# Last transform stage: four 64x64 quarters of the PE array and the plain 50 by 49 table, eight positions and 128 channels per call

## The chip, the cores and the metric

The kernel runs on one core of one Trainium2 chip. The metric is device time in microseconds (us); lower is better. A core has the matrix engine (PE, with its weight loads shown apart as PEld), the vector engine (DVE), the scalar engine (ACT), GpSimd (POOL), and SyncE (SP), whose queue issues the DMA transfers. PE reads SBUF and writes PSUM, from which ACT and DVE read.

## The reference

For each of 8 batches of 3136 positions by 256 channels, a real Fourier transform along the positions, a complex mix of the channels with a soft threshold, and the transform back; then a feed-forward block with a three-tap convolution and a gate.

```python
X = np.fft.rfft(x, axis=1)
Yr = Xr @ w_r - Xi @ w_i + b_r
Yi = Xr @ w_i + Xi @ w_r + b_i
Yr = np.sign(Yr) * np.maximum(np.abs(Yr) - 0.01, 0.0)      # Yi the same
y = np.fft.irfft(Yr + 1j * Yi, n=3136, axis=1)             # 8 x 3136 x 256
h = np.maximum(y @ w_in, 0.0)                              # 256 -> 1024
conv = sum(conv_w[k] * hp[:, k:k + 3136, :] for k in range(3))   # hp: h, one zero position each side
out = (h * sigmoid(conv)) @ w_out                          # 1024 -> 256
```

## The kernel before

3136 is 49 times 64, and the transform is done as two short ones, forward (stages 1 and 2) and back (stages 3 and 4). Stage 1 (L257, L274) and stage 2 (L301), the mix (L329), the threshold and stage 3 (L361) run first, for all batches, in about the first 535 us. Stage 3 leaves its result in DRAM: `sc2[b]` has 128 rows, 25 frequencies and 256 channels for batch b. Row 4j + 2o + c is position j (0 to 31) of half o (0 or 1), real (c = 0) or imaginary (c = 1).

Stage 4 (`stage4`, L502 to L516) is the last transform. For one j and one o it contracts 50 values (2 parts by 25 frequencies) with a fixed table of 50 by 49, which gives 49 output positions m; the position in the sequence is 64m + 32o + j. The kernel before does both halves o in one matmul: the table `i2` is 100 by 98 and block-diagonal (half of it is zero), and the stationary operand is `z2[:, j, 128 channels]`, 100 rows by 128 columns. A call covers four j and both halves of the channels: one transfer of 100 rows brings `z2` (L505), then 2 x 4 matmuls of 100 x 128 against 100 x 98 (L509) fill one PSUM bank per half of the channels, ACT casts the 784 results per partition to `yh` (L515), and DVE forms the rest `yl` (L516). A batch takes eight calls, all of them 64.

All matmuls of stages 1, 2 and 4 are plain fp32. In the trace each such matmul is two records on PE and two weight loads on PEld: stage 4 issues 512 matmuls and has 1024 records. The other matmuls are of split operands in fp32r (a high and a low part each), one record each.

Then the feed-forward block: 28 chunks of 896 positions, each in eight steps f of 128 hidden channels. `up` does 12 matmuls of 128 x 450 (L528), ACT and DVE make `gh` and `gl` from them (L530 to L543), and `down` does 21 matmuls of 128 x 256 (L556), four steps later. Stage 4 of batch 0 and two calls of batch 1 stand ahead of the first step; the other 54 calls are placed one at a time among the steps, by the loop's line `if todo and f in (1, 4, 7)`. `ps_s4` and `ps_h` share two PSUM buffers (tag `ps_h`), and `z2` has three buffers. From the feed-forward block on, and for stage 4, a scheduler with its own timeline orders the instructions of each engine; each engine then works in that order, and so does SP's queue.

Of the kernel before, what the change touches and what calls it, by code (L numbers as in the profile page):

```python
# [9 lines left out]
F32 = mybir.dt.float32  # L10
# [8 lines left out]
B, S, D, FF = 8, 3136, 256, 1024  # L19
R = 49  # L20
R2 = 64
U = 24
SP = 64
H = 32
# [5 lines left out]
P = 128  # L30
NT = D // P
# [4 lines left out]
def _tables():  # L36
    n = np.arange(R)
    n2 = np.arange(R2)
    u = np.arange(U + 1)

    f = np.zeros((R, 2, U + 1))
    ang = 2 * np.pi * ((n[:, None] * u[None, :]) % R) / R
    f[:, 0, :] = np.cos(ang)
    f[:, 1, :] = -np.sin(ang)
    fwd1 = np.zeros((R, 2, 2 * R))
    for h in range(2):
        for uu in range(1, U + 1):
            for c in range(2):
                fwd1[:, h, (uu - 1) * 4 + c * 2 + h] = f[:, c, uu]
        fwd1[:, h, 4 * U + h] = f[:, 0, 0]  # L50

    g = np.transpose(f, (1, 2, 0)).copy()
    g[:, 1:, :] *= 2.0
    g /= S
    g = np.roll(g, -1, axis=1)
    inv2 = np.zeros((2, 2 * (U + 1), R, 2))
    for i in range(2):
        inv2[i, :, :, i] = g.reshape(2 * (U + 1), R)
    fwd2 = np.zeros((2, R2, U + 1, 2, SP))
    inv1 = np.zeros((2, SP, U + 2, 2, R2))  # L60
    for uu in range(U + 1):
        at = (uu - 1) % (U + 1)
        for s in range(SP):
            k = uu + R * s
            th = 2 * np.pi * ((k * n2) % S) / S
            sn, cs = np.sin(th), np.cos(th)
            if uu == 0:
                if k > S // 2:
                    continue
                edge = k in (0, S // 2)  # L70
                if edge:
                    sn = np.zeros(R2)
                    cs = np.round(cs)
                w = 1.0 if edge else 2.0
                fwd2[0, :, at, 0, s] = cs
                fwd2[0, :, at, 1, s] = -sn
                inv1[0, s, at, 0, :] = w * cs
                inv1[1, s, at, 0, :] = -w * sn
            else:
                sg = 1.0 if k <= S // 2 else -1.0  # L80
                fwd2[0, :, at, 0, s] = cs
                fwd2[1, :, at, 0, s] = sn
                fwd2[0, :, at, 1, s] = -sn * sg
                fwd2[1, :, at, 1, s] = cs * sg
                inv1[0, s, at, 0, :] = cs
                inv1[0, s, at, 1, :] = sn
                inv1[1, s, at, 0, :] = -sg * sn
                inv1[1, s, at, 1, :] = sg * cs

    inv1[:, :, U + 1] = inv1[:, :, U]  # L90
    inv1[:, :, 1::2] = inv1[::-1, :, 1::2]

    return {
        "fwd1": fwd1.reshape(2 * R, 2 * R).astype(np.float32),
        "fwd2": fwd2.reshape(2 * R2, (U + 1) * 2 * SP).astype(np.float32),
        "inv1": inv1.reshape(2 * SP, U + 2, 2, 2, H).transpose(0, 1, 4, 3, 2).reshape(2 * SP, (U + 2) * 2 * R2).astype(np.float32),
        "inv2": inv2.reshape(4 * (U + 1), 2 * R).astype(np.float32),
    }


# [1 line left out]
def spectral_ffn_kernel(ctx: ExitStack, tc: tile.TileContext, x, w_r, w_i, b_r, b_i,  # L102
                        w_in, conv_w, w_out, fwd1, fwd2, inv1, inv2, out):
    nc = tc.nc
    K1, K2, KQ, KI = 2 * R, 2 * SP, 2 * R2, 4 * (U + 1)

    dram = ctx.enter_context(tc.tile_pool(name="dram", bufs=1, space=DRAM))
    sc1 = [dram.tile([K1, H, D], F32, name=f"sc1_{b}") for b in range(B)]
    sc2 = [dram.tile([KQ, U + 1, D], F32, name=f"sc2_{b}") for b in range(B)]

    cst = ctx.enter_context(tc.tile_pool(name="cst", bufs=1))


    i2 = cst.tile([KI, 112], F32, name="i2")[:, 0:K1]
    cw = cst.tile([P, 3, NF], F32, name="cw")
    win = [cst.tile([P, NT, FF], F32R, name=f"win_{q}") for q in range(2)]
    wout = [cst.tile([P, NF, D], F32R, name=f"wout_{q}") for q in range(2)]
# [363 lines left out]
    def pool(name, bufs=1, **kw):  # L481
        return ctx.enter_context(tc.tile_pool(name=name, bufs=bufs, reuse_waits="tile", **kw))

    zio, y_a = pool("zio", 3), pool("y_a")
# [3 lines left out]
    wk.tile([P, 24], F32, name="pad", bufs=1)  # L488
    psh, pso = pool("psh", 2, space=PSUM), pool("pso", space=PSUM)

    JG = 4
    NPC = H // JG

    def new_y(b):
        y = [(y_a, y_b)[b % 2].tile([P, NT, SW], F32R, name=nm) for nm in ("yh", "yl")]
        for q in y:
            qf = q.bitcast(F32)
            nc.vector.memset(qf[:, :, 0:1], 0.0)
            nc.vector.memset(qf[:, :, S + 1:S + 2], 0.0)
        return y  # L500

    def stage4(b, jg, y):  # L502

        z2 = zio.tile([KI, JG, D], F32, name="z2")
        nc.sync.dma_start(z2, sc2[b].rearrange("(j q) u e -> (q u) j e", q=4)[:, jg * JG:(jg + 1) * JG, :])  # L505
        ps = psh.tile([P, NT, 512], F32, name="ps_s4", tag="ps_h")
        for t in range(NT):
            for j in range(JG):
                nc.tensor.matmul(ps[:, t, j * K1:(j + 1) * K1], z2[:, j, t * P:(t + 1) * P], i2, start=(j == 0), stop=(j == JG - 1),  # L509
                                 skip_group_check=True)  # L510
        src = ps[:, :, 0:JG * K1].rearrange("p t (j m) -> p t m j", j=JG)

        def view(q):
            return q[:, :, 1:S + 1].rearrange("p t (m j) -> p t m j", j=H)[:, :, :, jg * JG:(jg + 1) * JG]
        nc.scalar.copy(view(y[0]), src)  # L515
        nc.vector.tensor_tensor(view(y[1]), src, view(y[0].bitcast(F32)), op=ALU.subtract)  # L516

    def up(f, halves):
        ps = psh.tile([P, 2, 512], F32, name="ps_h", tag="ps_h")
        w = slice(f * P, (f + 1) * P)  # L520
        for a, (y, c0) in enumerate(halves):
            mm = []
            for t in range(NT):
                mm.append((win[0][:, t, w], y[0][:, t, c0:c0 + CH + 2]))
                mm.append((win[0][:, t, w], y[1][:, t, c0:c0 + CH + 2]))
                mm.append((win[1][:, t, w], y[0][:, t, c0:c0 + CH + 2]))
            for n, (lt, rh) in enumerate(mm):
                nc.tensor.matmul(ps[:, a, 0:CH + 2], lt, rh, start=(n == 0), stop=(n == len(mm) - 1))  # L528
        h = hp.tile([P, 2, CH + 2], F32, name="h")
        nc.scalar.activation(h, ps[:, :, 0:CH + 2], AF.Relu)  # L530
        c = wk.tile([P, 2, CH], F32, name="c", bufs=3)
        if f in TAP_DVE:
            nc.vector.tensor_scalar_mul(c, h[:, :, 0:CH], cw[:, 0, f:f + 1])
        else:
            nc.scalar.mul(c, h[:, :, 0:CH], cw[:, 0, f:f + 1])  # L535
        for k in (1, 2):
            nc.vector.scalar_tensor_tensor(c, h[:, :, k:k + CH], cw[:, k, f:f + 1], c, op0=ALU.mult, op1=ALU.add)  # L537
        nc.scalar.activation(c, c, AF.Sigmoid)  # L538
        nc.vector.tensor_tensor(c, h[:, :, 1:CH + 1], c, op=ALU.mult)  # L539
        gh = wk.tile([P, 2, CH], F32R, name="gh", bufs=5)  # L540
        gl = wk.tile([P, 2, CH], F32R, name="gl", bufs=5)
        nc.scalar.copy(gh, c)  # L542
        nc.vector.tensor_tensor(gl, c, gh.bitcast(F32), op=ALU.subtract)  # L543
        return [q.rearrange("p a n -> p (a n)") for q in (gh, gl)]
# [32 lines left out]
    ys = {0: new_y(0)}  # L577
    for jg in range(NPC):
        with tc.high_priority(offset=HP):
            stage4(0, jg, ys[0])  # L580
    ys[1] = new_y(1)
    for jg in range(2):
        stage4(1, jg, ys[1])
    todo = [(1, jg) for jg in range(2, NPC)]
    gs, accs = {}, None
    n_st = NCH * NF
    for st in range(n_st + LAG):
        if st < n_st:
            ci, f = divmod(st, NF)
            hv = [divmod(2 * ci + a, NH) for a in range(2)]  # L590
            if f == 0:
                nb = hv[1][0] + 1
                if nb < B and nb not in ys and hv[0][0] == hv[1][0]:
                    ys[nb] = new_y(nb)
                    todo = [(nb, jg) for jg in range(NPC)]
            gs[st] = up(f, [(ys[b], a * CH) for b, a in hv])
            if todo and f in (1, 4, 7):
                b, jg = todo.pop(0)
                stage4(b, jg, ys[b])
        if st >= LAG:  # L600
            ci, f = divmod(st - LAG, NF)
            accs = down(ci, f, gs.pop(st - LAG), accs)
# [24 lines left out]
```

## Time and profile before

| | |
|---|---|
| median of 3 runs | 1760.06 us (1758.44 to 1760.09) |
| the profiled execution | 1759.99 us, span 1758.2 us, mean granted clock 0.990 |
| PE busy | 1721.6 us (98%) |
| DVE, ACT busy | 1472.0 us (84%), 1206.8 us (69%) |
| stage 4 on PE (L509) | 1024 records, busy 128.0 us; first 522.1 us, last 1568.4 us |
| stage 4 on ACT (L515), DVE (L516) | 64 each, 65.9 us and 67.4 us |
| loads of `z2` | 64 transfers of 400 KB |

The span runs from the first to the last instruction; the execution's own time is 1.8 us more. The matmuls overlap each other, so that the mean time of one (281 ns for stage 4) is far more than what one adds: the step from one start to the next is what counts. "x" is the number of records in a group. In the chain of waits a line of PE with "x16" is a stretch of so many records, with the time that they took.

### The profile page before, as it was taken

To read this page: it belongs to the slowest core of one execution; us is meant where nothing else is said; L and a number is where in the kernel's file an instruction comes from. 1 tells how busy PE (TensorE), PEld (TensorE's weight loads), DVE (VectorE), ACT (ScalarE), POOL (GpSimd) and SP (SyncE) were. 2 spreads that over 40 slices of the span, in tenths; PEclk is the share of its full clock that TensorE was granted. 3 is DMA by queue.
4 is the path that set the end of the run, shared out by engine and by line. 5 is a ranking of instruction groups with operands and counts; after the bars stand their busy time and mean duration, and the time that the engine had idled before them with its cause. 6 is when DMAs were issued, how large, how long until landed. Compare 5 with 4: busy or idle time off the path is not lost.

```text
span 1758.2 us, 28865 instructions
## 1 busy us (share of the span) xinstructions
PE 1721.6 (98%) x11872; PEld 1602.2 (91%) x11872; DVE 1472.0 (84%) x1757; ACT 1206.8 (69%) x1565; POOL 118.7 (7%) x54
## 2 busy tenths in 40 slices
PE   5999999999999999999999999999999999999999
PEld 2788888888988999999999999999999999999998
DVE  2778988889995988888888888888888888888887
ACT  2567677677665777677777777777777777777766
POOL 0122222222230000000000000000000000000000
PEclk8999999999998999999999999999999999999999
DMA  7877777767434110111111011111101111100001
GB/s 223 256 233 240 226 230 237 232 204 234 141 104 126 42 48 22 41 50 50 41 50 50 22 40 50 50 40 50 50 22 41 50 50 41 50 22 22 22 22 43
DMA packets 108305, 165.48 MB, mean 94 GB/s; under 512 B 8492, under 2 KB 86316, under 8 KB 108174
## 3 DMA queue, kind: packets, MB, share of 16 engines
q1 hardware_dynamic: 108174, 163.64, 29.4%
q8 instruction: 94, 1.54, 0.4%
q14 instruction: 37, 0.30, 0.1%
HBM read 86.02 MB, written 77.59 MB: 93 GB/s over the span
## 4 chain that ended last, share of the span: by engine, by line
PE 93%; DMA 2%; DVE 2%; issue 1%; ACT 0%; SPq 0%; DVEq 0%; ACTq 0%
PE ps_h L528 31%; PE acc L556 31%; PE ps_mx L329 11%; PE ps_s L509 6%; PE ps_s L257 5%; PE ps_s L301 5%; PE ps_s L361 3%; DMA t<-in_fwd_dram 1%; DMA z<-sc 1%; DVE v L337 0%; DMA sc<-a 0%; DVE p L333 0%; DMA sc<-ha 0%; DVE fl L307 0%; DVE v L348 0%
## 5 line engine op out<-in xcount | busy, mean ns | idle before, releaser
L556 PE MATMUL acc<-wout,gh 128*128 128x256 f32 x3136 | 567.4, 280 | 0.0
L528 PE MATMUL ps_h<-yh,win 128*128 128x450 f32 x1792 | 550.6, 368 | 0.0
L537 DVE SCALAR_TENSOR_TENSOR c<-h,cw,c 128x896 f32<-128x896 f32 x448 | 512.9, 1147 | 38.9 <-ACT c L535 37.3
L556 PEld LDWEIGHTS acc<-wout,gh 128*128 128x128 f32 x3136 | 490.1, 188 | 5.1
L556 PE MATMUL acc<-wout,gl 128*128 128x256 f32 x1568 | 437.4, 280 | 0.0
L530 ACT ACTIVATE h<-ps_h 128x900 f32<-128x900 f32 x224 | 207.4, 926 | 261.1 <-PE ps_h L528 261.1
L528 PEld LDWEIGHTS ps_h<-yh,win 128*128 128x128 f32 x1792 | 339.4, 189 | 26.1 <-DVE yl L516 0.4
L528 PE MATMUL ps_h<-yl,win 128*128 128x450 f32 x896 | 329.7, 368 | 0.0
L543 DVE TENSOR_TENSOR gl<-c,gh 128x896 fp32r<-128x896 f32 x224 | 243.0, 1088 | 76.3 <-ACT gh L542 74.7
L556 PEld LDWEIGHTS acc<-wout,gl 128*128 128x128 f32 x1568 | 293.8, 188 | 0.6
L539 DVE TENSOR_TENSOR c<-h,c 128x896 f32<-128x896 f32 x224 | 243.1, 1086 | 48.2 <-ACT c L538 48.2
L542 ACT CAST gh<-c 128x896 fp32r<-128x896 f32 x224 | 211.0, 942 | 70.2 <-DVE c L539 68.3
L538 ACT ACTIVATE c<-c 128x896 f32<-128x896 f32 x224 | 213.0, 951 | 8.2 <-DVE c L537 4.4
L329 PE MATMUL ps_mx<-wmix_hi,fl 128*128 128x256 f32 x600 | 185.2, 309 | 2.8 <-DVE fl L311 2.8
L329 PE MATMUL ps_mx<-wmix_hi,fh 128*128 128x256 f32 x600 | 183.7, 306 | 0.7 <-DVE v L337 0.6
L528 PEld LDWEIGHTS ps_h<-yl,win 128*128 128x128 f32 x896 | 169.4, 189 | 11.0
L535 ACT ACTIVATE c<-h,cw 128x896 f32<-128x896 f32 x168 | 176.1, 1048 | 2.2 <-DVE gl L543 0.2
L329 PE MATMUL ps_mx<-wmix_lo,fh 128*128 128x256 f32 x600 | 168.6, 281 | 0.0
L351 POOL TENSOR_TENSOR sl<-v,sh 128x1024 fp32r<-128x1024 f32 x50 | 118.5, 2370 | 410.7 <-PE ps_s L361 254.1
L337 DVE TENSOR_TENSOR v<-ps_mx,p 64x512 f32<-64x512 f32 x200 | 137.4, 687 | 2.9
L301 PEld LDWEIGHTS ps_s<-t,a 128*128 128x128 f32 (+1 forms) x800 | 99.7, 198 | 39.6 <-issue 28.8
L509 PEld LDWEIGHTS ps_s<-i,z 100*128 100x128 f32 x1024 | 128.1, 198 | 5.8 <-issue 3.0
(84 smaller groups left out, 1959.2 us busy)
## 6 DMA issues: line engine op xcount, KB each, us to landing
z<-sc SPq DMA_DIRECT2D x64, 400.0 KB
xr<-in_x_dram SPq DMA_DIRECT2D x63, 392.0 KB
a<-sc SPq DMA_DIRECT2D x48, 512.0 KB
sc<-z SPq DMA_DIRECT2D x48, 512.0 KB
out_dram<-o SPq DMA_DIRECT2D x27, 896.0 KB
sc<-a SPq DMA_DIRECT2D x56, 392.0 KB
sc<-ha SPq DMA_DIRECT2D x8, 392.0 KB
win_bits<-in_moe_w_in_dram SPq DMA_DIRECT2D x4, 512.0 KB
```

The source lines that it names most:

```text
L301: nc.tensor.matmul(ps[:, k], a2[0:rows, k, t * P:(t + 1) * P], t2[0:rows, u, :], start=(k == 0), stop=(k == UG - 1), skip_group_check=True)
L329: nc.tensor.matmul(ps[c][:, k, :], lt, rh, start=(n == 0), stop=(n == len(mm) - 1))
L509: nc.tensor.matmul(ps[:, t, j * K1:(j + 1) * K1], z2[:, j, t * P:(t + 1) * P], i2, start=(j == 0), stop=(j == JG - 1), skip_group_check=True)
L528: nc.tensor.matmul(ps[:, a, 0:CH + 2], lt, rh, start=(n == 0), stop=(n == len(mm) - 1))
L530: nc.scalar.activation(h, ps[:, :, 0:CH + 2], AF.Relu)
L535: nc.scalar.mul(c, h[:, :, 0:CH], cw[:, 0, f:f + 1])
L537: nc.vector.scalar_tensor_tensor(c, h[:, :, k:k + CH], cw[:, k, f:f + 1], c, op0=ALU.mult, op1=ALU.add)
L538: nc.scalar.activation(c, c, AF.Sigmoid)
L539: nc.vector.tensor_tensor(c, h[:, :, 1:CH + 1], c, op=ALU.mult)
L542: nc.scalar.copy(gh, c)
L543: nc.vector.tensor_tensor(gl, c, gh.bitcast(F32), op=ALU.subtract)
L556: nc.tensor.matmul(acc[m // 2][:, m % 2, :], lt[:, sl], rh[:, f, :], start=(f == 0 and n == 0 and m % 2 == 0), stop=(f == NF - 1 and n == ...
```

## The change

Stage 4 uses the table once, 50 by 49, held twice in SBUF: in partitions 0 to 49 and in 64 to 113. A call now covers eight j and one half of the channels (128), so that a batch still has eight calls. `z2` has half o = 0 in partitions 0 to 49 and o = 1 in 64 to 113, and is brought by two transfers of 50 rows. For each j there are four matmuls: for each half o (rows 0 or 64 on) and each 64 of the 128 channels (PSUM partitions 0 or 64 on), 50 x 64 against 50 x 49. Each thus names one quarter of the array. A call has 32 matmuls in place of 8. Half o = 0 writes one PSUM bank and o = 1 the other. The casts and the differences still have 784 elements per partition, in runs of eight in place of four.

```diff
-    inv2 = np.zeros((2, 2 * (U + 1), R, 2))
-    for i in range(2):
-        inv2[i, :, :, i] = g.reshape(2 * (U + 1), R)
+    inv2 = np.zeros((2, R2, R))
+    inv2[:, 0:2 * (U + 1)] = g.reshape(2 * (U + 1), R)
...
-    i2 = cst.tile([KI, 112], F32, name="i2")[:, 0:K1]
+    i2 = cst.tile([P, 112], F32, name="i2")[:, 0:R]
...
-    JG = 4
-    NPC = H // JG
+    JG = 8
+    NPC = H // JG * NT
...
-    def stage4(b, jg, y):
-
-        z2 = zio.tile([KI, JG, D], F32, name="z2")
-        nc.sync.dma_start(z2, sc2[b].rearrange("(j q) u e -> (q u) j e", q=4)[:, jg * JG:(jg + 1) * JG, :])
-        ps = psh.tile([P, NT, 512], F32, name="ps_s4", tag="ps_h")
-        for t in range(NT):
-            for j in range(JG):
-                nc.tensor.matmul(ps[:, t, j * K1:(j + 1) * K1], z2[:, j, t * P:(t + 1) * P], i2, start=(j == 0), stop=(j == JG - 1),
-                                 skip_group_check=True)
-        src = ps[:, :, 0:JG * K1].rearrange("p t (j m) -> p t m j", j=JG)
+    def stage4(b, n, y):
+
+        js, t = slice(n // NT * JG, (n // NT + 1) * JG), n % NT
+        z2 = zio.tile([P, JG, P], F32, name="z2")
+        z2v = sc2[b].rearrange("(j o c) u e -> o (c u) j e", o=2, c=2)
+        for o in range(2):
+            nc.sync.dma_start(z2[o * R2:o * R2 + KI], z2v[o, :, js, t * P:(t + 1) * P])
+        ps = psh.tile([P, 2, 512], F32, name="ps_s4", tag="ps_h")
+        for j in range(JG):
+            for o in range(2):
+                rows = slice(o * R2, o * R2 + KI)
+                for c in range(2):
+                    half = slice(c * R2, (c + 1) * R2)
+                    nc.tensor.matmul(ps[half, o, j * R:(j + 1) * R], z2[rows, j, half], i2[rows, :], start=(j == 0), stop=(j == JG - 1),
+                                     skip_group_check=True)
+        src = ps[:, :, 0:JG * R].rearrange("p o (j m) -> p o m j", j=JG)
```

The order of PE in the middle of the feed-forward block, before: `ps_s` is `ps_s4`, `acc` the output of `down`, and "x8" eight equal instructions in a row.

```order
L528 MATMUL ps_h<-yh,win_79 128x450
L528 MATMUL ps_h<-yh,win_78 128x450
L528 MATMUL ps_h<-yl,win_78 128x450
L528 MATMUL ps_h<-yh,win_79 128x450
L509 MATMUL ps_s_12473<-i_76,z_12471 128x98 x8
L556 MATMUL acc_12224<-wout_80,gl 128x256
L556 MATMUL acc_12225<-wout_80,gh 128x256
```

The same place in the changed kernel (L514 was L509, L533 was L528, L561 was L556):

```order
L533 MATMUL ps_h<-yh,win_79 128x450
L533 MATMUL ps_h<-yh,win_78 128x450
L533 MATMUL ps_h<-yl,win_78 128x450
L533 MATMUL ps_h<-yh,win_79 128x450
L514 MATMUL ps_s_12640<-i_76,z_12637 64x49 x32
L561 MATMUL acc_12397<-wout_80,gh 128x256
L561 MATMUL acc_12397<-wout_81,gh 128x256
```

A call is still one stretch without other matmuls in it, now of 32, between matmuls that name the whole array. In both kernels the 64 calls make 57 such stretches: three ahead of the feed-forward block, of two, two and six calls, and 54 of one call.

The order of SP's queue in the same part, before (`z` is `z2`, `sc_2` the result of stage 3 for batch 2):

```order
L505 DMA z_7527<-sc_2_67 100x4x256
L569 DMA out_dram<-o 128x7x256
L505 DMA z_7684<-sc_2_67 100x4x256
L505 DMA z_7839<-sc_2_67 100x4x256
L569 DMA out_dram<-o 128x7x256 x2
L505 DMA z_7944<-sc_2_67 100x4x256
```

And in the changed kernel (L507 was L505, L574 was L569):

```order
L507 DMA z_7927<-sc_2_67 50x8x128 x2
L574 DMA out_dram<-o 128x7x256
L507 DMA z_8109<-sc_2_67 50x8x128 x2
L507 DMA z_8289<-sc_2_67 50x8x128 x2
L574 DMA out_dram<-o 128x7x256 x2
L507 DMA z_8419<-sc_2_67 50x8x128 x2
```

Each load of `z2` is two issues in place of one, at the same place of the queue between the stores of the output.

More of the change, by code (lines that the diff above doesn't have):

```diff
@@ L96, in _tables @@
         "inv1": inv1.reshape(2 * SP, U + 2, 2, 2, H).transpose(0, 1, 4, 3, 2).reshape(2 * SP, (U + 2) * 2 * R2).astype(np.float32),
-        "inv2": inv2.reshape(4 * (U + 1), 2 * R).astype(np.float32),
+        "inv2": inv2.reshape(P, R).astype(np.float32),
     }
@@ L104, in spectral_ffn_kernel @@
     nc = tc.nc
-    K1, K2, KQ, KI = 2 * R, 2 * SP, 2 * R2, 4 * (U + 1)
+    K1, K2, KQ, KI = 2 * R, 2 * SP, 2 * R2, 2 * (U + 1)
     dram = ctx.enter_context(tc.tile_pool(name="dram", bufs=1, space=DRAM))
@@ L500, in new_y @@
         return y
-    def stage4(b, jg, y):
-        z2 = zio.tile([KI, JG, D], F32, name="z2")
-        nc.sync.dma_start(z2, sc2[b].rearrange("(j q) u e -> (q u) j e", q=4)[:, jg * JG:(jg + 1) * JG, :])
-        ps = psh.tile([P, NT, 512], F32, name="ps_s4", tag="ps_h")
-        for t in range(NT):
-            for j in range(JG):
-                nc.tensor.matmul(ps[:, t, j * K1:(j + 1) * K1], z2[:, j, t * P:(t + 1) * P], i2, start=(j == 0), stop=(j == JG - 1),
-                                 skip_group_check=True)
-        src = ps[:, :, 0:JG * K1].rearrange("p t (j m) -> p t m j", j=JG)
+    def stage4(b, n, y):
[13 more added lines that the diff above has]
+        src = ps[:, :, 0:JG * R].rearrange("p o (j m) -> p o m j", j=JG)
         def view(q):
-            return q[:, :, 1:S + 1].rearrange("p t (m j) -> p t m j", j=H)[:, :, :, jg * JG:(jg + 1) * JG]
+            return q[:, t, 1:S + 1].rearrange("p (m o j) -> p o m j", o=2, j=H)[:, :, :, js]
         nc.scalar.copy(view(y[0]), src)
```

## The prediction

> **What bounds the kernel now.** I began with the busy shares and the chain of work that ended last.
>
> ```profile
> PE 1721.6 (98%) x11872; PEld 1602.2 (91%) x11872; DVE 1472.0 (84%) x1757; ACT 1206.8 (69%) x1565; POOL 118.7 (7%) x54
> ...
> PE 93%; DMA 2%; DVE 2%; issue 1%; ACT 0%; SPq 0%; DVEq 0%; ACTq 0%
> PE ps_h L528 31%; PE acc L556 31%; PE ps_mx L329 11%; PE ps_s L509 6%; PE ps_s L257 5%; PE ps_s L301 5%; PE ps_s L361 3%; DMA t<-in_fwd_dram 1%; DMA z<-sc 1%; DVE v L337 0%; DMA sc<-a 0%; DVE p L333 0%; DMA sc<-ha 0%; DVE fl L307 0%; DVE v L348 0%
> ```
>
> PE makes 93% of the chain, and stage 4 (L509) 6% of it, about 105 us. Whether that holds where stage 4 runs is read from the stretches of the span: ahead of the feed-forward block, its body, and the end.
>
> ```profile
> 522.00:552.00 30.00, 26.39 (x183) 25.73 (x184) 10.96 (x15) 12.97 (x13) 3.81 (x2) 0.82 0.57 174
> ...
> 542.00:552.00 10.00, 10.00 (x47) 10.00 (x48) 2.18 (x3) 2.01 (x2) 0.00 (x0) 0.50 0.50 127
> ...
> 552.00:1568.00 1016.00, 1016.00 (x6995) 978.49 (x6993) 870.22 (x874) 724.88 (x850) 0.00 (x0) 1.00 0.13 42
> ```
>
> The columns are PE, PEld, DVE, ACT and POOL, then the granted clock, the DMA share and GB/s. From 552 to 1568 us, where 54 of the 64 calls stand, PE has no idle time in 1016 us at clock 1.00. DVE has 146 us to spare there, ACT 291. What a call costs PE there goes straight into the time. The ten calls from 522 to 552 us stand among waits, and in the last ten microseconds at half the clock.
>
> **What a call of stage 4 costs now.** From the chain, in order of time (start, length, what), two calls of stage 4 and stretches of other lines:
>
> ```profile
> 305.08 0.86 PE ps_s L257 x2
> 305.94 1.79 PE ps_s L301 x16
> ...
> 610.23 2.45 PE ps_h L528 x12
> 612.69 1.76 PE ps_s L509 x16
> 614.45 2.71 PE acc L556 x23
> ...
> 629.19 1.76 PE ps_s L509 x16
> ```
>
> A call is 16 records in 1.76 us, 110 ns each; 64 calls are 64 x 1.76 = 112.6 us. What sets 110 ns? Stage 2 (L301) streams 128 columns in place of 98 and needs almost the same, 1.79 / 16 = 112 ns, while stage 1 (L257), with 512 columns, needs 0.86 / 2 = 430 ns, or 0.84 ns per column. At 0.84 ns stage 4's 98 columns would take 82 ns. So the stream is not what paces stage 4: its weight load is, 128 columns in 110 ns or 0.86 ns per column. The load times agree:
>
> ```profile
> L509 PEld LDWEIGHTS ps_s<-i,z x1024: 186/192/333, 522.0 to 1568.4; 100*128 100x128 f32 x171
> ...
> L257 PEld LDWEIGHTS ps_s<-xr,f x224: 161/164/285, 39.3 to 440.5; 98*98 98x98 f32 x112
> ```
>
> Median 192 ns for 128 columns and 164 for 98 is 28 ns for 30 columns, near 0.9 ns per column. The number of rows doesn't enter. In the half-clock stretch above, 47 records take 10.00 us, 213 ns each: the pace scales with the array's clock, so issuing instructions isn't what binds at 110 ns.
>
> **The change part by part.**
>
> *Weight loads.* A call had 16 loads of 128 columns, 2048 columns. It now has 32 matmuls, 64 records, and 64 loads of 64 columns: 4096 columns. One load is 64 x 0.86 = 55 ns; one stream of 49 columns is 49 x 0.84 = 41 ns, so the load stays the longer of the two. Nothing in this trace runs two quarters at once, so the cost is bounded by how many work together: one at a time, 64 x 55 = 3.52 us; two, 1.76 us; four, 0.88 us. I take two. Each fp32 matmul is two records on the same quarter (1024 records for 512 matmuls), and matmuls start in the program's order in every stretch I looked at. The second record has to wait 55 ns for its own quarter's load; only it and the next quarter's first record can overlap. That gives 32 steps of 55 ns, 1.76 us: as much as before, nothing gained, nothing lost.
>
> *Entering and leaving the quarters.* The trace has one case in which the array isn't used whole: stage 2 of frequency 0 has 64 rows (L301, 64*128). It stands between the same neighbours as a usual one of 128 rows, and I compare the two, from the last start of L361 to the second start of L329.
>
> ```profile
> 456.03 0.27 PE L361 MATMUL ps_s<-sh,i_lo 128*128 128x256 f32 x1
> 456.23 2.05 PE L301 MATMUL ps_s<-t,a 64*128 64x128 f32 x16
> ...
> 458.44 0.28 PE L329 MATMUL ps_mx<-wmix_lo,fh 128*128 128x256 f32 x1
> ...
> 504.90 0.27 PE L361 MATMUL ps_s<-sh,i_lo 128*128 128x256 f32 x1
> 505.01 1.95 PE L301 MATMUL ps_s<-t,a 128*128 128x128 f32 x16
> ...
> 506.92 0.28 PE L329 MATMUL ps_mx<-wmix_lo,fh 128*128 128x256 f32 x1
> ...
> L301 PEld LDWEIGHTS ps_s<-t,a x16: 183/188/188, 456.2 to 457.9; 64*128 64x128 f32 x16
> L301 PE MATMUL ps_s<-t,a x16: 272/272/374, 456.2 to 458.0; 64*128 64x128 f32 x16
> ```
>
> With 64 rows 458.44 - 456.03 = 2.41 us, with 128 rows 506.92 - 504.90 = 2.02 us: 0.39 us more for the same 16 records. It lies at the two ends: the first load waits for the last matmul of the other kind (0.20 us from 456.03 to 456.23, against 0.11), and so again on leaving. I read it as the array emptying whenever the split changes. Stage 4 is now 57 such stretches: 57 x 0.39 = 22.2 us. Lower bound: nothing, if the 0.39 us is a matter of that one place. Upper: twice that, as columns are split too.
>
> The Trainium skill has this as a rule: "TensorEngine Tiling (Array Packing)", Key Properties, says that changing the tiling mode drains the engine, while changing only the tile does not. It speaks against this change as the row does, and gives no figure; by the row it is 22 us.
>
> *Transfers.* Each call has two issues of 200 KB in place of one of 400 KB, in pieces of half the length. Of the ten loads ahead of the feed-forward block, two stand on the chain:
>
> ```profile
> 525.65 4.71 DMA z<-sc
> ...
> 535.73 6.04 DMA z<-sc
> ...
> L505 SPq DMA_DIRECT2D z<-sc x64: 275/275/862, 477.5 to 1524.1; - x64
> ```
>
> Below, nothing; above, a doubling of both, 10.8 us, if the number of pieces alone counted. I take one more issue of 0.28 us for each and a little for the pieces: 1 us. In the body loads lie three buffers ahead, calls being 16.5 us apart in the rows above (612.69 and 629.19), and PE is never idle; if that cover went, each call would cost some 5 us. The issue itself keeps SP 0.28 us longer, and behind it stand stores of the output, which nothing waits for in the body.
>
> *ACT and DVE.* The same 784 elements per partition in 64 casts and 64 differences, 65.9 and 67.4 us; runs of eight in place of four. I take no change; both engines have room in the body, and if each call's cast and difference took 0.3 us more it would still be hidden. The shared PSUM buffers are handed on as before. The table's load moves 25 KB in the first part, off the chain.
>
> Sum: 1759.99 + 0 + 22.2 + 1 = **1783 us** against the profiled execution; the median is 1760.06, so it stands for both.
>
> **The rivals.**
>
> *Loads one at a time* (slower, more). If the quarters don't load together, a call is 3.52 us, 1.76 more: 64 x 1.76 = 112.6, and 1760 + 112.6 + 23 = 1896 us. For it: every load in this trace follows the one before at the pace of its columns, though each pair is free to run ahead. In between: if the two row halves load together but the two column halves, which read the same rows, don't, then the eight records of one j take 6 x 55 = 330 ns in order, a call 2.64 us, 64 x 0.88 = 56 more: 1839 us.
> The skill's page "TensorE: Matmul & The Clock Gate", Part 3, says that a load overlaps matmuls in flight only when the row group differs. The 64-row stretch doesn't bear that out as a general rule: its 16 records of one row group took 2.05 us, though a load (188 ns) and a matmul (272 ns) one after the other would take 7 us. For column halves nothing here shows it.
>
> *Four quarters at once* (faster). If order doesn't hold the quarters back, a call's records take 0.88 us, and with the ends 1.27 against 1.76. In the body 54 x 0.88 = 47.5 saved; ahead of it the ten calls wait for transfers and for PSUM anyway, and I count nothing: 1760 - 47.5 + 22.2 = 1735 us. It decides once a record takes less than (1.76 - 0.39) / 64 = 21 ns. For it: four quarters share neither array cells nor, across o, a PSUM bank. Against: two records in a row name the same quarter.
> The tiling page's rule that different tiles can load and multiply in parallel would, taken fully, give this.
>
> *No price at the ends*: two quarters at a time without the 22 us, 1761 us, no difference.
>
> *Worse*: loads not hidden under streams in a quarter, 55 + 41 = 96 ns per record, 6.1 us per call, some 2060 us.
>
> **How the numbers follow.** Two at a time 0.36; one at a time 0.23; row halves alone 0.11; four at once 0.20; no price at the ends 0.06; worse 0.04. The likeliest gives 1783 us, its own range 1765 to 1805 (the ends at half to nearly double the price). The whole range is 1737 to 1900: it leaves out the worse case and most of the four at once below, about two in ten. A measurement of this kernel tells about 0.2% (3.5 us) from no change: faster 0.20, same 0.05, slower 0.75.
>
> **What would show it.** On PE, L514 is the line: in the chain a stretch of 64 records would take about 1.8 us (two at once), 3.5 (one), 0.9 (four). The ends show as 0.2 us from the last start of L533 to the first load of L514 beyond what is usual, and again before L561. From 552 us on PE should stay without idle time, L533 and L561 at their old pace (2.45 / 12 = 204 and 2.71 / 23 = 118 ns); if ACT or DVE appear as what PE waits for there, the part on evacuation is wrong. If loads of `z2` end waits in the body, the part on transfers is. The prediction falls if the body's length changes by other than 54 times the difference per call.

## The result: faster by 21 us, where 23 us slower was forecast

| | before | changed |
|---|---|---|
| median | 1759.53 us (4 runs) | 1738.55 us (4 runs, 1738.14 to 1739.72) |
| ratio | | 0.9883, 95% interval 0.9865 to 0.99 |
| span of the profiled execution | 1758.2 us | 1736.3 us |
| first matmul of the feed-forward block, in the span | 552.1 us | 555.7 us |
| from there to the end | 1206.1 us | 1180.6 us |

The prediction was wrong: it said 1783 us, and 0.75 for slower. The time lies at the bottom of its range, beside the rival of four quarters at once (1735 us); the range holds it only because it was drawn down to 1737 us, not because a term of the sum gave it.

The page of the changed kernel, its head and the chain of work that ended last:

```profile
PE 1690.5 (97%) x14944; PEld 1552.5 (89%) x14944; DVE 1471.0 (85%) x1757; ACT 1198.4 (69%) x1565; POOL 118.6 (7%) x54
...
PE 93%; DMA 4%; DVE 2%; issue 1%; ACT 1%; SPq 0%; DVEq 0%; ACTq 0%
PE acc L561 32%; PE ps_h L533 32%; PE ps_mx L328 11%; PE ps_s L256 5%; PE ps_s L300 5%; PE ps_s L514 4%; PE ps_s L360 3%; DMA z<-sc 1%; DMA wm_raw<-in_w_i_dram 1%; DMA t<-in_fwd_dram 1%; DVE v L336 0%; DMA sc<-a 0%; PE ps_s1h L273 0%; DMA xr<-in_x_dram 0%; DVE p L332 0%
```

PE has 3072 records more and is busy for 31 us less. Stage 4 is 4% of the chain where it was 6%, and DMA 4% where it was 2%.

One call in the body, in the order of time on PE (start, length, what), before the change and after it:

```profile
612.32 0.37 PE L528 MATMUL ps_h<-yh,win 128*128 128x450 f32 x1
612.52 1.92 PE L509 MATMUL ps_s<-i,z 100*128 100x98 f32 x16
...
614.55 0.28 PE L556 MATMUL acc<-wout,gl 128*128 128x256 f32 x1
```

```profile
780.76 0.36 PE L533 MATMUL ps_h<-yh,win 128*128 128x450 f32 x1
781.05 1.15 PE L514 MATMUL ps_s<-i,z 50*64 50x49 f32 x64
782.13 0.50 PE L561 MATMUL acc<-wout,gh 128*128 128x256 f32 x2
782.47 0.28 PE L561 MATMUL acc<-wout,gl 128*128 128x256 f32 x1
```

From the last start of `up` to the third start of `down`: 2.23 us before, 1.71 after, 0.52 us less. 54 calls make 28 us. The 64 records start within 0.93 us (their last start is 781.98): one every 14.5 ns, four in 58 ns. A load of 64 columns was put at 55 ns; so all four quarters work at once, each at the pace of its own loads (that it is the load and not the stream is shown below, by the row halves).

Part of the 28 us was given back ahead of the feed-forward block. The chain of the changed kernel there (pieces under 0.5 us are left out, here and in the chains further down):

```profile
520.14 2.15 PE ps_s L514 x125
523.08 5.38 DMA z<-sc
528.51 3.08 PE ps_s L514 x95
532.36 5.66 DMA z<-sc
538.06 3.08 PE ps_s L514 x96
541.44 4.68 DMA z<-sc
546.17 2.87 PE ps_s L514 x88
549.32 4.49 DMA z<-sc
553.85 1.95 PE ps_s L514 x60
555.80 6.32 PE ps_h L533 x24
```

The same part before the change:

```profile
522.30 3.35 PE ps_s L509 x31
525.65 4.71 DMA z<-sc
530.50 2.00 PE ps_s L509 x16
532.50 1.45 PE ps_s L361 x12
533.94 1.78 PE ps_s L509 x16
535.73 6.04 DMA z<-sc
541.90 10.53 PE ps_s L509 x48
552.43 6.19 PE ps_h L528 x24
```

Four loads of `z2` end waits where two did: 20.2 us of the chain in place of 10.8. PE's own stretches of stage 4 are shorter there too, 13.1 us in place of 17.7. From the first start of stage 4 to the first of `up` it takes 555.7 - 520.1 = 35.6 us, against 552.1 - 522.1 = 30.0. The windows of this stretch and of the body (PE, PEld, DVE, ACT, POOL, granted clock, DMA share, GB/s):

```profile
540.00:556.00 16.00, 9.99 (x294) 9.12 (x289) 4.78 (x7) 4.46 (x6) 0.00 (x0) 0.50 0.48 111
556.00:1546.00 990.00, 988.50 (x9558) 933.42 (x9560) 870.12 (x874) 717.46 (x850) 0.00 (x0) 1.00 0.15 44
```

PE is busy for 10 of 16 us there, at half the clock, and the DMA engines for half of the time: neither is the limit. The granted clock also fell earlier than before, 0.67 from 530 to 540 us where it was 1.00; what share of the loss that has, these runs don't separate. The body has 1.5 us of idle PE, one wait of the first `down` for `gh`, behind a chain of ACT and DVE from 562 to 567 us: in the new order it stands behind 36 matmuls of `up`, where it stood behind 60.

So the span: 28 us less in 54 calls, about 2.5 us back in the body (the wait of 1.5 us, and 1 us that I can't place), 5.6 us back ahead of it, and 2.0 us less because stage 4 starts at 520.1 in place of 522.1 us, in a part that the change doesn't touch (the kernels below start between 518.0 and 521.5). -28 + 2.5 + 5.6 - 2.0 = -21.9, and the spans differ by 21.9; that the sum closes is no check, as the 2.5 us is what was left over (1206.1 - 1180.6 = 25.5).

### The profile page after: what moved, and what is told of

Its sections match the earlier page's. It is cut to its first block, busy times and chain, and to the rows that moved or that the text cites. A ratio compares the mean times of both kernels' runs of the same rounds, so it can differ in the third digit from the quotient of the medians.

```text
span 1736.3 us, 35086 instructions
## 1 busy us (share of the span) xinstructions
PE 1690.5 (97%) x14944; PEld 1552.5 (89%) x14944; DVE 1471.0 (85%) x1757; ACT 1198.4 (69%) x1565; POOL 118.6 (7%) x54
## 4 chain that ended last, share of the span: by engine, by line
PE 93%; DMA 4%; DVE 2%; issue 1%; ACT 1%; SPq 0%; DVEq 0%; ACTq 0%
PE acc L561 32%; PE ps_h L533 32%; PE ps_mx L328 11%; PE ps_s L256 5%; PE ps_s L300 5%; PE ps_s L514 4%; PE ps_s L360 3%; DMA z<-sc 1%; DMA wm_raw<-in_w_i_dram 1%; DMA t<-in_fwd_dram 1%; DVE v L336 0%; DMA sc<-a 0%; PE ps_s1h L273 0%; DMA xr<-in_x_dram 0%; DVE p L332 0%
## 5 line engine op out<-in xcount | busy, mean ns | idle before, releaser
L561 PE MATMUL acc<-wout,gh 128*128 128x256 f32 x3136 | 567.7, 281 | 1.5 <-ACT gh L547 1.5
L533 PE MATMUL ps_h<-yh,win 128*128 128x450 f32 x1792 | 550.4, 368 | 0.0
L561 PEld LDWEIGHTS acc<-wout,gh 128*128 128x128 f32 x3136 | 491.3, 188 | 10.4 <-ACT gh L547 1.9
L561 PE MATMUL acc<-wout,gl 128*128 128x256 f32 x1568 | 437.0, 280 | 0.0
L533 PEld LDWEIGHTS ps_h<-yh,win 128*128 128x128 f32 x1792 | 339.2, 189 | 25.8
L533 PE MATMUL ps_h<-yl,win 128*128 128x450 f32 x896 | 329.7, 368 | 0.0
L561 PEld LDWEIGHTS acc<-wout,gl 128*128 128x128 f32 x1568 | 293.6, 188 | 0.1
L533 PEld LDWEIGHTS ps_h<-yl,win 128*128 128x128 f32 x896 | 169.6, 189 | 11.1
L328 PEld LDWEIGHTS ps_mx<-wmix_hi,fh 128*128 128x128 f32 x600 | 113.2, 189 | 19.1 <-issue 17.4
```

The lines of the kernel that those rows point to most:

```text
L328: nc.tensor.matmul(ps[c][:, k, :], lt, rh, start=(n == 0), stop=(n == len(mm) - 1))
L561: nc.tensor.matmul(acc[m // 2][:, m % 2, :], lt[:, sl], rh[:, f, :], start=(f == 0 and n == 0 and m % 2 == 0), stop=(f == NF - 1 and n == ...
```

## The experiments

### Does the order of the quarters matter?

The prediction took it that matmuls start in the program's order, so that a record that waits for its load holds back the next quarter. Two kernels change the order of a call's 32 matmuls alone: runs of eight positions on one quarter, and runs of two.

```diff
-        for j in range(JG):
+        for j0 in range(0, JG, 8):       # the second kernel: 2
             for o in range(2):
                 rows = slice(o * R2, o * R2 + KI)
                 for c in range(2):
                     half = slice(c * R2, (c + 1) * R2)
-                    nc.tensor.matmul(ps[half, o, j * R:(j + 1) * R], ...)
+                    for j in range(j0, j0 + 8):
+                        nc.tensor.matmul(ps[half, o, j * R:(j + 1) * R], ...)
```

> Stage 4 of the changed kernel with its 32 matmuls per call in another order: all eight positions of one quarter, then the next quarter. Theory 1 (order): four quarters work at once only because neighbours in the program's order name different quarters. Then 16 records in a row name one quarter, a call takes about 64 x 58 ns + 0.34 us = 4.1 us in place of 1.27, and the time is 1890 to 1915 us. Theory 2 (a queue for each quarter): the order doesn't matter, a call stays at 1.27 us and the time at 1738 us.

> The same with runs of two positions per quarter (four records in a row on one quarter). Theory 1 (order): only the ends of a run overlap, 12 steps of 58 ns for 16 records, a call 2.8 + 0.34 = 3.1 us, the time about 1840 us; if the two records of a matmul don't stand next to each other in the order, half of that, 1.9 us and 1770 us. Theory 2 (queues): 1.27 us per call, 1738 us.

Measured: 1916.78 us with runs of eight and 1752.86 us with runs of two, one run each (before on the same chip 1756.75). A call in the chain of waits, of runs of eight and of runs of two:

```profile
957.41 3.29 PE ps_s L515 x64
```

```profile
947.59 1.18 PE ps_s L515 x61
```

The changed kernel's call is 1.08 us in that view. With runs of eight the quarters work nearly one after the other. With runs of two nearly nothing is lost. Between the last start of `up` and the second of `down` a call takes 1.60 us in the changed kernel, 1.70 with runs of two and 3.80 with runs of eight (medians of 51 calls, from the starts in the traces). Neither theory fits as it was put: the order matters for long runs and not for short ones. The starts within one call with runs of two show why; they are worked out from the trace, in ns after the call's first start on PE:

```text
0 13 27 40   94 107 121 134   152 166 179 192   211 224 237 251
```

Four records start within 40 ns, though in the program's order the first four are all of one quarter. One quarter can't start a record before the one ahead has had its 58 ns, so these four are on four quarters: three records of the first quarter stood waiting while matmuls behind them went on to the others. With runs of eight, the windows of the call's first microseconds, of L515 alone:

```profile
1021.92:1022.66 0.74, 0.74 (x13) 0.74 (x13) 1.00 0.00 0
1022.66:1023.40 0.74, 0.74 (x20) 0.74 (x18) 1.00 0.00 0
```

13 records in the first 0.74 us, 57 ns each: one quarter alone. Then a second quarter joins, with 13 of the first quarter's 16 records started and 3 still to come. Both kernels say the same: about three records per quarter can wait without holding back what is behind them. The spacing agrees: quarters start 7 ns apart where two records stand on each (starts 0, 7, 13, 20 in the changed kernel) and 13 ns apart where four do, as if a record needed 3.3 ns to be handed to its quarter. That each quarter has a queue of this depth is what I conclude; the trace shows starts, no queue and no quarter's name.

The time with runs of two is 14 us above the changed kernel although a call costs only 0.10 us more (54 x 0.10 = 5.4). The rest is ahead of the feed-forward block, which begins at 563.4 us of the span, 44.7 us after stage 4's first start in place of 35.6.

### Rows, columns, or both?

One kernel splits the rows alone (50 x 128 against 50 x 49), and one the columns alone, in the kernel before (100 x 64 against the block-diagonal 100 x 98).

```diff
-                for c in range(2):
-                    half = slice(c * R2, (c + 1) * R2)
-                    nc.tensor.matmul(ps[half, o, j * R:(j + 1) * R], z2[rows, j, half], i2[rows, :], ...)
+                nc.tensor.matmul(ps[:, o, j * R:(j + 1) * R], z2[rows, j, :], i2[rows, :], ...)
```

```diff
-                nc.tensor.matmul(ps[:, t, j * K1:(j + 1) * K1], z2[:, j, t * P:(t + 1) * P], i2, ...)
+                for c in range(2):
+                    half = slice(c * R2, (c + 1) * R2)
+                    nc.tensor.matmul(ps[half, t, j * K1:(j + 1) * K1], z2[:, j, t * P + c * R2:t * P + (c + 1) * R2], i2, ...)
```

> The changed kernel with only the row halves split: 50 x 128 against 50 x 49, 16 matmuls and 32 records per call, loads of 128 columns (112 ns). If the two row halves work at once: 16 x 112 ns = 1.79 + 0.34 = 2.13 us per call, 0.86 more than the changed kernel, 1785 to 1793 us. If they work one after the other: 3.9 us per call, 1885 to 1905 us.

> The kernel before with only the columns split: 100 x 64 against the block-diagonal 100 x 98, 16 matmuls and 32 records per call. The stream of 98 columns (about 86 ns) is then longer than the load of 64 (55 ns). If the two column halves work at once: 16 x 86 ns = 1.38 + 0.34 = 1.72 us per call against 2.11 - 0.32 = 1.79 before, so 1755 us. If their loads share one path: 1.76 + 0.34 = 2.1 us, 1777 us. One after the other: 3.1 us, 1830 to 1843 us.

Measured: 1796.59 and 1750.58 us, one run each (before 1756.75). A call in the chain, of row halves and of column halves:

```profile
785.77 1.92 PE ps_s L512 x32
```

```profile
791.61 1.50 PE ps_s L511 x32
```

Rows: 32 loads of 128 columns one after the other would take 32 x 112 = 3.6 us; the stretch takes 1.92, so two row halves load at once. Columns: 32 streams of 98 columns one after the other would take 32 x 86 = 2.75 us; it takes 1.50, so two column halves work at once too, although both read the same rows of SBUF. The starts also tell what paces a half: the row halves repeat every 112 ns and the quarters every 58 ns, with the same streams of 49 columns, so there it is the load of 128 or 64 columns; the column halves repeat every 84 ns, which is the stream of 98. Per call, between the same two starts as above, 2.44 and 2.01 us, less 0.32 of `up` and `down` themselves: 2.12 (expected 2.13) and 1.69 (expected 1.72). The row halves' time is a little above its range, again by the part ahead of the feed-forward block (45.8 us). So in each split the two halves work at once. Alone, neither gains much on the call before, which takes 2.11 us between the same starts: the column halves gain 0.10 us, the row halves lose 0.33 us. The changed kernel, with both, takes 1.60 us.

### What do the ends of a stretch cost?

An extra full-array matmul stands once in the middle of each call, where it makes two more changes of the split, and once behind it, where it makes none. Its result is in PSUM columns that nobody reads.

```diff
         for j in range(JG):
+            if j == 4:        # the second kernel: behind the loops
+                nc.tensor.matmul(ps[:, 0, 448:512], win[0][:, 0, 0:P], win[1][:, 0, 0:R2], start=False, stop=False, ...)
             for o in range(2):
```

> The changed kernel with one more matmul in the middle of each call: a full 128 x 128 against 64 columns, into PSUM columns that nobody reads (computed beyond the reference). It splits each call's stretch in two, so that the array changes its split twice more. If changing the split costs 0.34 us for a pair of changes, a call takes 0.34 + about 0.12 us more, 2.06 us between its neighbours in place of 1.60, and the time is about 1738 + 54 x 0.46 + some = 1765 us. If the ends cost nothing by themselves: 1745 us.

> The same extra matmul behind each call, where the whole array is used next anyway: no more changes of the split. Its own cost alone, about 0.12 us per call, 1.72 us between the neighbours, about 1746 us. The difference to the kernel with it in the middle is the price of two changes.

Measured: 1761.3 us in the middle and 1751.23 at the end, one run each. A call with the extra matmul in the middle (L511), and one with it at the end (L516), on PE:

```profile
947.39 0.37 PE L535 MATMUL ps_h<-yh,win 128*128 128x450 f32 x1
947.69 0.68 PE L516 MATMUL ps_s<-i,z 50*64 50x49 f32 x32
948.30 0.30 PE L511 MATMUL ps_s<-win,win 128*128 128x64 f32 x1
948.53 0.68 PE L516 MATMUL ps_s<-i,z 50*64 50x49 f32 x32
949.14 0.51 PE L563 MATMUL acc<-wout,gh 128*128 128x256 f32 x2
```

```profile
1101.58 0.36 PE L534 MATMUL ps_h<-yh,win 128*128 128x450 f32 x1
1101.87 1.15 PE L514 MATMUL ps_s<-i,z 50*64 50x49 f32 x64
1102.95 0.30 PE L516 MATMUL ps_s<-win,win 128*128 128x64 f32 x1
1103.09 0.48 PE L562 MATMUL acc<-wout,gh 128*128 128x256 f32 x2
```

32 records take 0.46 us of pace (32 x 14.5 ns), but from the start of the first half to that of the next it is 948.53 - 947.69 = 0.84 us. Medians from the last start of `up` to the second of `down`: 1.60 us without the extra matmul, 1.70 with it at the end, 1.97 in the middle. So the matmul costs 0.10 and two changes 0.27 us. By the times it is less: (1761.3 - 1751.2) / 54 = 0.19 us per call. The bodies alone differ by 1200.3 - 1191.5 = 8.8 us, and in them PE waits 4.3 us with the matmul at the end and 1.3 us with it in the middle; without these waits it is 11.8 us, 0.22 us per call. The ends are real, at 0.2 to 0.3 us for the two (with any load in it that nothing covers); the prediction had 0.39 from the case with 64 rows. 54 calls pay 10 to 15 us for them.

### Where the 5.6 us ahead of the feed-forward block went

In the order of the kernel before, only the first two of the ten calls there have their matmuls interleaved one by one; in the changed kernel, four pairs of calls have. A pair frees both of its buffers at its end, and with three buffers the third call then stands interleaved with a fourth that is still to be loaded. The casts of ACT, which follow each call's last matmul, show it: before 526.1 and 527.0 us, then one at a time; after 523.9 and 524.7, 531.6 and 532.4, 541.1 and 541.9, 549.0 and 549.8, then two single ones. Three causes were open: this order, the shorter pieces of the transfers (512 B in place of 1 KB), and the number of buffers. Two kernels take the pairs apart, by a priority of its own for each call of batch 0, and by holding PE to the program's order there:

```diff
     for jg in range(NPC):
-        with tc.high_priority(offset=HP):
+        with tc.high_priority(offset=HP * (NPC - jg)):
             stage4(0, jg, ys[0])
```

```diff
     for jg in range(NPC):
-        with tc.high_priority(offset=HP):
+        with tc.manual_schedule(engines={mybir.EngineType.PE}):
             stage4(0, jg, ys[0])
...
     for jg in range(2):
-        stage4(1, jg, ys[1])
+        with tc.manual_schedule(engines={mybir.EngineType.PE}):
+            stage4(1, jg, ys[1])
```

> The changed kernel with another priority for each of the eight calls of batch 0, so that PE's order has the calls ahead of the feed-forward block one after the other and not two interleaved; nothing else is changed. If loads that wait for a pair of calls to free two buffers at once make the 5.7 us there, buffers now come free one by one: the first matmul of the feed-forward block at 545 to 549 us of the span in place of 555.7, 1728 to 1732 us. If the smaller pieces are the limit: 1738 us.

> The changed kernel with PE held to the order in which the program states the ten calls ahead of the feed-forward block, without the raised priority: calls one after the other too, but the first starts and the last steps of stage 3 stand in another order. Theory of the buffers: as the kernel before this one, 1728 to 1734 us. Theory of the pieces: 1738 us.

Two more have calls of four positions and both halves of the channels, with pieces of 1 KB; the second has the priorities too:

```diff
-        z2 = zio.tile([P, JG, P], F32, name="z2")
+        z2 = zio.tile([P, JG, D], F32, name="z2")          # JG = 4
...
-            nc.sync.dma_start(z2[o * R2:o * R2 + KI], z2v[o, :, js, t * P:(t + 1) * P])
+            nc.sync.dma_start(z2[o * R2:o * R2 + KI], z2v[o, :, js, :])
...
-        nc.scalar.copy(view(y[0]), src)
-        nc.vector.tensor_tensor(view(y[1]), src, view(y[0].bitcast(F32)), op=ALU.subtract)
+        for t in range(NT):
+            nc.scalar.copy(view(y[0], t), src[:, :, t])
+            nc.vector.tensor_tensor(view(y[1], t), src[:, :, t], view(y[0].bitcast(F32), t), op=ALU.subtract)
```

> The changed kernel with calls of four positions and both halves of the channels, as before the change: the same two transfers of 200 KB per call, but in pieces of 1 KB in place of 512 B; as a cast cannot have the shape that this needs, ACT and DVE evacuate each call in two instructions. The pairs of calls ahead of the feed-forward block stay interleaved. Theory of the pieces: that part 5 us shorter, 1733 us. Theory of the buffers: 1738 us, or somewhat more for the evacuation.

> Both of these: 1 KB pieces and calls one after the other. If each has its own effect, 1725 to 1728 us; if only the buffers count, 1730 us.

| | median, ratio to before (95%) | first matmul of `up` |
|---|---|---|
| changed kernel | 1738.55, 0.9883 (0.9865 to 0.99) | 555.7 us |
| own priorities | 1736.37, 0.9876 (0.9861 to 0.9891) | 552.4 us |
| program's order | 1733.13, 0.9854 (0.9837 to 0.987) | 549.6 us |
| 1 KB pieces | 1738.16, 0.9882 (0.9867 to 0.9897) | 555.4 us |
| 1 KB pieces, own priorities | 1737.97, 0.9883 (0.9868 to 0.9898) | 555.5 us |

Pieces of 1 KB bring no gain: loads still end waits, and as long ones. (ACT and DVE evacuate each call in two instructions in these two kernels, which could hide a small gain.) Two of the waits in that kernel's chain:

```profile
523.51 5.06 DMA z<-sc
...
532.22 5.25 DMA z<-sc
```

Taken apart, the calls start the block 3.3 us sooner by priority and 6.1 us sooner in the program's order. Of the 6.1 us, 2.1 lie ahead of stage 4, which starts at 518.0 us in that profile in place of 520.1. From stage 4's first start to `up` it takes 32.8 us by priority and 31.6 in the program's order, where it takes 35.7 in the changed kernel and 30.0 before. The kernel with the priorities is held up by something else: all eight calls now stand ahead of the last steps of stage 3, and a store of stage 3's result ends a wait just before `up`.

```profile
547.14 3.95 DMA sc<-z
551.41 0.95 DVE yl L521
552.40 7.04 PE ps_h L533 x24
```

With pieces of 1 KB the same priorities gain nothing, 36.0 us. Its eight calls follow one another too, and the same store ends the wait before `up`, at 553.2 us in place of 551.1; why its calls take longer is open.

The kernel in the program's order has the lowest median of all. Against the changed kernel its profile is 5.4 us shorter in span; the two ratios' intervals just overlap, so the times alone don't settle that step. Its chain still has loads of 6.9 and 6.6 us:

```profile
531.84 6.90 DMA z<-sc
538.78 1.97 PE ps_s L514 x60
541.08 6.62 DMA z<-sc
547.75 1.95 PE ps_s L514 x60
549.69 6.97 PE ps_h L533 x24
```

Two more kernels were meant for the question of the buffers, the changed kernel with a fourth buffer of `z2`, and with one load for two calls in two buffers of twice the size. Neither fits into SBUF, so neither has a time. The fourth buffer then went into the kernel in the program's order: to make room beside the feed-forward block's tile `c`, which has three buffers, a control has two of `c`, and a little less padding, and the next has the fourth buffer too.

```diff
-    SW = 3168
+    SW = 3140
...
-        c = wk.tile([P, 2, CH], F32, name="c", bufs=3)
+        c = wk.tile([P, 2, CH], F32, name="c", bufs=2)
...
-    zio, y_a = pool("zio", 3), pool("y_a")
+    zio, y_a = pool("zio", 4), pool("y_a")       # not in the control
```

> The kernel with PE held to the program's order ahead of the feed-forward block, with two buffers in place of three for the feed-forward block's tile c and 28 columns less of padding in the y tiles, to make room. Control for the next kernel: 1733 us if the third buffer of c was of no use, more if PE now waits in the body.

> The same with four buffers of z2 in place of three. If ahead of the feed-forward block each buffer's round (load of 5.5 to 6.6 us, then PE 1.9 us at half the clock) sets the pace, ten calls at (6.5 + 1.9) / 4 = 2.1 us in place of 2.8 us: about 6 us less than the control, 1727 us. If the transfers are limited by what the DMA engines move there, or by PSUM, no change against the control.

Measured: 1745.65 us for the control and 1743.73 with four buffers (0.9925, 0.9908 to 0.9942; 0.9918, 0.9903 to 0.9933). The fourth buffer brings the first `up` from 552.7 to 548.4 us of the span, 4.3 us sooner, some 4 us of the expected 6, and the profiled span is 3.9 us shorter; in the medians the gain isn't clear of their spread. It is one profile each, and the control itself starts `up` 3.0 us later than the kernel in the program's order (552.7 and 549.6 us), though stage 4's calls there are the same and in the same order. `c` with two buffers costs some 10 us in the body (1191.6 in place of 1181.2 us): PE then waits 5.9 us for `gh`.

```profile
PE acc L561 <- ACT gh L547: 5.9, 3, 3.6
```

So the order of the pairs made most of the loss ahead of the feed-forward block, 3 to 4 of the 5.6 us by stage 4's stretch to `up`; longer pieces bring no gain, with the reserve made above; and the number of buffers has a part in what remains, by one pair of profiles. The rest of the loss, and what each load's 4.5 to 7 us consists of, stay open; the DMA engines were busy for 0.35 to 0.76 of the time there, in windows of 10 us from 520 to 550 us of the changed kernel and the first four of these.

## Why the prediction was wrong

- **What bounds the kernel**: right. PE is idle for 1.5 of 990 us of the body after the change, and what a call costs there went nearly straight into the time: 25.5 us of 28.
- **The pace of the loads**: right. 0.86 ns per column gave 55 ns for 64; measured 58 ns per step (0.93 us / 16).
- **How many quarters work together**: here it failed. The step was "The second record has to wait 55 ns for its own quarter's load; only it and the next quarter's first record can overlap." It rested on matmuls that start in the program's order in every stretch of the trace; but in all of these the array was one piece or one half, and a waiting record had nothing to let pass. The runs of two and of eight show that records for other quarters start while about three of one quarter wait. So 16 steps, not 32: 0.93 us in place of 1.76, which is -0.83 us per call and -45 us in 54 calls, where the sum had 0.
- **The rivals**: four quarters at once had 0.20, and 1.27 us per call; measured 1.71 us less 0.44 for `up` and `down` (0.205 and 2 x 0.117), 1.27. Nothing in the trace spoke on whether quarters hold each other up, so the chance should have been split more evenly. Row halves alone (0.11) is ruled out by the column halves, which work at once too. The rule of the Trainium skill in "TensorEngine Tiling (Array Packing)", Key Properties, that different tiles can load and multiply in parallel, is borne out (64 records in 0.93 us). The rule of the Trainium skill in "TensorE: Matmul & The Clock Gate", Part 3, that a load overlaps matmuls in flight only when the row group differs, is not: the column halves, on the same rows, worked at once (1.50 us in place of 2.75).
- **The ends**: right in kind, too large. 0.2 to 0.3 us in place of 0.39 by the extra matmul in the middle. From the call itself, 1.27 - 0.93 = 0.34 us is left, which also holds the first load that nothing covers.
- **Transfers**: the sign was right and the size wrong: 5.6 us in place of 1. The pieces that I priced show no effect when they are made longer. What I left out is in PE's order: pairs of calls interleaved, so that buffers came free in twos, 3 to 4 us of the 5.6.
- **ACT and DVE**: the cast and the difference became a little shorter, not equal: 65.9 to 58.4 us and 67.4 to 61.8 us over 64 calls, with runs of eight. It's hidden in the body.

```profile
L521 DVE TENSOR_TENSOR yl<-ps_s,yh 128x784 fp32r<-128x784 f32 x64 | 61.8, 971 | 18.9 <-ACT yh L520 18.9
L520 ACT CAST yh<-ps_s 128x784 fp32r<-128x784 f32 x64 | 58.4, 920 | 21.1 <-PE ps_s L514 21.1
```

## What to carry to other kernels

Where a block-diagonal or short table leaves half of the array multiplying zeros, and the pace is that of the weight loads, quarters of the array are worth trying even though they double the columns to load: four loads run side by side, as long as neighbours in the order name different quarters (runs of four records cost 0.10 us per call here, runs of 16 cost 2.2). Price the ends of each stretch (0.2 to 0.3 us here) and make stretches long enough for it. And read the order of the part where buffers are few: that a scheduler interleaves two calls took back 3 to 4 us of the 28.

## What the runs showed of the hardware

- Four quarters of 64 x 64 start records 7 ns apart and each repeats every 58 ns: 64 loads of 64 columns and 64 streams of 49 in 0.93 us, 14.5 ns per record, where the whole array needs 110 ns for a load of 128 columns.
- Records don't start in the program's order once they name different quarters: with four in a row on each, four start within 40 ns. 16 in a row on one quarter hold the next back for 0.74 us, until 13 have started, so about three can wait (worked out from the starts).
- With plain fp32, row halves and column halves each work at once by themselves: 32 records in 1.92 and 1.50 us, where one after the other would take 3.6 and 2.75.
- A stretch of quarters between full-array matmuls pays 0.2 to 0.3 us for its two ends.
